# Sliding-window attention and gated MLP on one NeuronCore: 64-key score tiles, batched P V, and Q/K transposed on chip

## The chip, the core and the metric

The kernel runs on one NeuronCore of one Trainium2 chip. It is a whole transformer block in one launch: adaptive layer norm, attention in a sliding window, a second layer norm and a gated MLP, over 2048 tokens of width 640. The metric is device time in microseconds, the median of several runs. Names used below: TensorE (PE) multiplies matrices, PSUM is the memory it writes, in eight banks of 512 fp32 columns by 128 partitions; ScalarE (ACT) does the exponentials, VectorE (DVE) and GpSimd (POOL) work element by element, and SyncE (SP) issues the transfers.

## The reference

All values are bf16. `x` is 1 x 2048 x 640, there are 32 heads of 20 dimensions, and each query sees itself and the 255 tokens before it.

```python
mod = (silu(c) @ w_mod).reshape(1, 6, 1, -1)          # sa, ca, ga, sb, cb, gb
h = layernorm(x) * (1 + ca) + sa
x = x + ga * A(h, wqkv, wo)
h = layernorm(x) * (1 + cb) + sb
x = x + gb * B(h, w_gate, w_up, w_down)

def A(x, wqkv, wo):                                   # H = 32, Dh = 20, W = 256
    q, k, v = split(x @ wqkv)                         # by head
    scores = einsum('bhqd,bhkd->bhqk', q, k) * Dh ** -0.5
    mask = (idx[:, None] - idx[None, :] >= 0) & (idx[:, None] - idx[None, :] < W)
    p = softmax(where(mask, scores, -1e9))
    return merge(einsum('bhqk,bhkd->bhqd', p, v)) @ wo

def B(x, w_gate, w_up, w_down):                       # F = 1536
    return (sigmoid(x @ w_gate) * (x @ w_up)) @ w_down
```

## The kernel before

Every operation is recorded with an estimated duration, what it reads and writes, and a priority. A list scheduler then fixes the order of each engine's instructions ahead of time, and the order is emitted with semaphore waits. Buffers come from pools; a tile takes a slot when its first operation is placed. So the trace has one line for all untiled matmuls (L513) and one for the tiled ones (L514).

Pools and banks that matter here:

```python
CHUNKS = [2, 2, 4, 4, 4]                  # queries of a chunk, in blocks of 128
p_hT  = sbpool("hT", 2, [128, NDT, 512])  # x normalized and modulated, transposed
p_stg = sbpool("stg", 3, [128, 512])
p_QT  = sbpool("QT", 3, [128, 4, 512])
p_KT  = sbpool("KT", 4, [128, 4, 512])
p_V   = sbpool("V", 10, [128, H * VW + 10])
p_E   = sbpool("E", 4, [128, 4, 512])     # exponentials
p_S = Pool("S", [psum("S0", [128, 4, 512])])               # four banks: one score set
p_O = Pool("O", [psum("O0", [128, 512])])                  # one bank: P V
p_M = Pool("M", [psum(f"M{i}", [128, 512]) for i in range(3)])   # three banks: all else
```

Q and K are projected 512 tokens at a time with the dimensions on the partitions, then written to DRAM and read back so that four heads of a group lie at partitions 0, 32, 64 and 96:

```python
for mt in mts:                                        # 128 of the 640 dimensions
    pairs = [(ps, w[:, kt, mt * 128:(mt + 1) * 128], hT[cc].ap[:, kt, :]) for kt in range(NDT)]
    pe_chain(ps, 512, pairs, ...)
    evac(s, ps)                                       # PSUM to SBUF, ScalarE or VectorE
    dma(d[mt * 128:(mt + 1) * 128, :], s)             # to DRAM
for hh in halves:
    for j in range(4):                                # back, one head in four
        dma(t.ap[32 * j:32 * j + DH, :, :],
            d.rearrange("(g r) c -> r g c", r=4 * DH)[j * DH:(j + 1) * DH, 4 * hh:4 * hh + 4, :])
```

Attention goes group by group of four heads. A set is up to four pieces of 128 keys by 128 queries, so 512 columns in each of four banks. Scores use four row tiles of the array, P V four column tiles, directly after each other with a lag of two sets:

```python
for (kb, q0, n) in st:                                # scores: keys on 128 partitions
    for j in range(4):
        mm(Sp.ap[:, j, off:off + n * 128], kt.ap[32 * j:32 * j + DH, gl, keys of kb],
           qt.ap[32 * j:32 * j + DH, gl, queries], tp=(32 * j, 0))
activation(E.ap[:, :, 0:ncol], Sp.ap[:, :, 0:ncol], ACT.Exp, scale=SM_SCALE)
# diagonal and far blocks, on GpSimd:
affine_select(ap, ap, pattern=[[0, 4], [1, 128]], compare_op=ALU.is_ge, fill=0.0, ...)
for (kb, q0, n) in st:                                # P V
    for j in range(4):
        mm(O.ap[32 * j:32 * j + 32, oc:oc + n * 128], V[kb].ap[:, h * VW:h * VW + 32],
           E.ap[:, j, off:off + n * 128], tp=(0, 32 * j))
```

A full O bank is normalized on VectorE (transpose, reciprocal of the row sums, product, transpose back), goes to DRAM and comes back as the transposed input of the output projection. The MLP of a chunk computes gate and up for 128 of the 1536 hidden dimensions at a time, over all tokens of the chunk:

```python
for ft in range(NFT):
    for ps, w in ((pg, wg), (pu, wu)):
        pe_chain(ps, W, [(ps.ap[:, 0:W], w[:, kt, ft * 128:(ft + 1) * 128], h2.ap[:, kt, 0:W])
                         for kt in range(NDT)])
    activation(sg, pg, ACT.Tanh, scale=0.5)           # ScalarE
    scalar_tensor_tensor(hv(ft), sg, 1.0, pu, ALU.add, ALU.mult)   # VectorE
```

Of the kernel before, what the change touches and what calls it, by code (L numbers as in the profile page):

```python
# [13 lines left out]
D = 640  # L14
# [5 lines left out]
NG = H // 4  # L20
EPS = 1e-5
# [3 lines left out]
SWITCH = 0.094  # L25
ENGATTR = {"pe": "tensor", "act": "scalar", "dve": "vector", "pool": "gpsimd", "sp": "sync"}
ENGS = ("pe", "act", "dve", "pool", "sp")

# [44 lines left out]
class Op:  # L73
    __slots__ = ("engs", "eng", "fn", "dur", "lat", "deps", "succ", "tiles", "prio", "seq", "nleft", "ready", "start",
                 "end", "mode", "done", "key", "val", "signal", "nbytes", "k", "tmin", "isdma", "tag", "waits")


class Prog:
    def __init__(self, nc):
        self.nc = nc  # L80
        self.ops = []
        self.seq = 0

    def op(self, eng, fn, dur, reads=(), writes=(), prio=50.0, lat=0.06, nbytes=0, k=16, tmin=0.0, extra=(), tag="", hold=(), mode=0):
        o = Op()
        o.mode = mode
        o.engs = eng if isinstance(eng, tuple) else (eng,)
# [7 lines left out]
        o.isdma = nbytes > 0  # L95
        o.nbytes = nbytes
        o.k = k
# [42 lines left out]

    def schedule(self):
# [26 lines left out]

        for o in self.ops:
            if o.nleft == 0:  # L170
                arm(o)
        n = len(self.ops)
        placed = 0
        while placed < n:
            best = None
            for e in ENGS:
# [5 lines left out]
                for o in c.values():  # L182
                    st = max(free[e] + (SWITCH if e == "pe" and o.mode != pemode else 0.0), o.ready)
                    ok = True
                    for t in o.tiles:
                        if t.slot is None:
                            bs = None
                            for s in range(len(t.pool.tenant)):
                                rt = slot_time(t.pool, s)
                                if rt is not None and (bs is None or rt < bs):  # L190
                                    bs = rt
                            if bs is None:
                                ok = False
                                break
                            st = max(st, bs)
                        else:
                            for x in t.prev:
                                st = max(st, x.end + x.lat)
                    if ok:
                        lst.append((st, o))  # L200
                        if tmin is None or st < tmin:
                            tmin = st
                if not lst:
                    continue
                eps = 0.13 if e == "pe" else 0.04
                pick = min((x for x in lst if x[0] <= tmin + eps), key=lambda x: (x[1].prio, x[1].seq))
                ent = (pick[0], e, pick[1])
                if best is None or ent[0] < best[0]:
                    best = ent
# [8 lines left out]
            for t in o.tiles:  # L218
                if t.slot is None:
                    bs = None  # L220
                    for s in range(len(t.pool.tenant)):
                        rt = slot_time(t.pool, s)
                        if rt is not None and (bs is None or rt < bs[0]):
                            bs = (rt, s)
                    s = bs[1]
                    ten = t.pool.tenant[s]
                    t.prev = list(t.pool.init[s]) if ten is None else list(ten.rel)
                    t.slot = s
                    t.pool.tenant[s] = t
# [4 lines left out]
            free[e] = st + dur  # L234
            if o.isdma:
                s0 = max(st + dur + 1.2, bw)
                move = o.nbytes / 340e3
                bw = s0 + move
                o.end = s0 + max(move, o.nbytes / (o.k * 22e3)) + 0.9
# [12 lines left out]
            for t in o.tiles:  # L252
                t.left -= 1
                if t.left == 0:
                    last = {}
                    for x in t.ops:
                        if x.isdma:
                            last[x] = x
                        else:
                            last[x.eng] = x  # L260

# [12 lines left out]
    def emit(self):  # L274
# [6 lines left out]
        for e in ENGS:  # L281
            for o in self.order[e]:
# [4 lines left out]
                for d in ds:  # L287
                    if d is o:
                        continue
                    if d.eng == e and not d.isdma:  # L290
                        assert pos[d] < pos[o], (d.tag, o.tag)
                        if e in ("pe", "sp"):
                            continue
# [59 lines left out]
def c_pool(n):  # L353
    return 0.22 + n / 1150.0


def c_pe(n):
    return max(n, 64) / 2400.0 + 0.003


PVLAG = 2
MW = 100
CHUNKS = [2, 2, 4, 4, 4]


def build(nc, A_x, A_wqkv, A_wo, B_x, B_w_gate, B_w_up, B_w_down, c, w_mod, out, S=2048):
    NB = S // 128
    NCH = S // 512
# [18 lines left out]
    ident = sb("ident", [128, 128])  # L387
    c_col = sb("c_col", [128, NDT])
# [9 lines left out]
    p_x1 = sbpool("x1", 8, [128, D])  # L398
    p_hT = sbpool("hT", 2, [128, NDT, 512])
    p_h2 = sbpool("h2T", 1, [128, NDT, 512])  # L400
    p_stg = sbpool("stg", 3, [128, 512])
    p_QT = sbpool("QT", 3, [128, 4, 512])
    p_KT = sbpool("KT", 4, [128, 4, 512])
    p_V = sbpool("V", 10, [128, H * VW + 10])
    p_E = sbpool("E", 4, [128, 4, 512])
# [4 lines left out]
    p_oT = sbpool("oT", 1, [128, NDT, 512])  # L410
    p_big = sbpool("big", 1, [128, 6400])
    p_sig = sbpool("sig", 2, [128, 512], F32)
    p_st = sbpool("st", 3, [128, 64], F32)

    p_S = Pool("S", [nc.alloc_psum_tensor("S0", [128, 4, 512], F32)])
    p_O = Pool("O", [nc.alloc_psum_tensor("O0", [128, 512], F32)])
    p_M = Pool("M", [nc.alloc_psum_tensor(f"M{i}", [128, 512], F32) for i in range(3)])

    def R(name):
        return Res(name)  # L420

    R_wq, R_wk, R_wv, R_ident, R_ccol, R_cth, R_siluc, R_silubc = (
        R(n) for n in ("wq", "wk", "wv", "ident", "ccol", "cth", "siluc", "silubc"))
    R_wo = R("wo")
# [3 lines left out]
    R_mA, R_shB, R_scB, R_gbc, R_mh = R("mA"), R("shB"), R("scB"), R("gbc"), R("mh")  # L428
# [554 lines left out]
```

The softmax here doesn't subtract the row's maximum and nothing guards it: scores larger than these inputs give would overflow.

## Time and profile before

The median time is 378.63 us (378.45 to 379.73). The profiled execution took 378.4 us.

| | busy us | share of the span | instructions |
|---|---|---|---|
| TensorE matmuls | 344.5 | 91% | 3198 |
| TensorE weight loads | 172.9 | 46% | 3198 |
| ScalarE | 223.0 | 59% | 207 |
| VectorE | 218.8 | 58% | 471 |
| GpSimd | 177.0 | 47% | 281 |

| group | count | mean ns of one |
|---|---|---|
| exponential of 2048 elements, ScalarE | 80 | 1876 |
| exponential of 1536 elements, ScalarE | 8 | 1448 |
| mask selection of 512 elements, GpSimd | 240 | 662 to 665 |
| transposes of O, fp32 and back in bf16, VectorE | 32 and 32 | 714 and 707 |
| gate or up matmul of 512 columns | 360 | 386 to 387 |
| gate or up matmul of 256 columns | 240 | 273 |

How to read it: matmuls are pipelined, so the duration of one is longer than its distance to the next, and a busy TensorE isn't TensorE at its peak. The page cuts the span into 40 slices of 9.46 us and prints a digit for each, the busy share in tenths; a row of the same kind gives the clock that TensorE was granted. A line of a group names the source line, the engine, the operation, output <- input and the shapes. A line of the timeline gives start, duration, engine, operation and count, and in brackets how long the engine had been idle and what released it. Buffer numbers are left out of names.

### The profile page before, as it was taken

The numbers are of one execution on the slowest core, as the hardware profiler recorded it, in microseconds if no ns is written. First come the engines' busy times: TensorE is split into PE (matmuls) and PEld (weight loads), VectorE is DVE, ScalarE is ACT, GpSimd is POOL, SyncE is SP. The second block draws the span as 40 slices with busy tenths as digits, with TensorE's granted clock in tenths as the row PEclk, the third lists the DMA queues.
The fourth block names the chain that finished last, engine by engine and source line by source line (L and its number), as shares of the span: only waits on it lengthen the run. The fifth ranks groups of instructions, "written<-read, shape, count | busy, mean of one in ns | idle before, by whom it ended". The sixth has DMA issues, their size and how long they took to land.

```text
span 378.4 us, 8381 instructions
## 1 busy us (share of the span) xinstructions
PE 344.5 (91%) x3198; PEld 172.9 (46%) x3198; DVE 218.8 (58%) x471; ACT 223.0 (59%) x207; POOL 177.0 (47%) x281
## 2 busy tenths in 40 slices
PE   5796697678999799999999879999999999989996
PEld 2453243123445244655556423353554345744464
DVE  4354175767877755556886545397564638433332
ACT  1352366776888769878888767878778421012210
POOL 8111144679676845666668574667567300000000
PEclk9999699579999889999999969999999999999999
DMA  6999799976365042034203511200343020320001
GB/s 215 338 303 192 232 309 373 291 195 197 95 149 144 17 126 75 29 94 101 89 19 88 112 47 36 88 2 20 45 114 87 2 87 3 74 66 0 0 19 52
DMA packets 52887, 42.81 MB, mean 113 GB/s; under 512 B 22768, under 2 KB 49648, under 8 KB 52848
## 3 DMA queue, kind: packets, MB, share of 16 engines
q1 hardware_dynamic: 52848, 42.29, 41.0%
q8 instruction: 25, 0.41, 0.4%
q14 instruction: 14, 0.11, 0.1%
HBM read 27.20 MB, written 10.49 MB: 100 GB/s over the span
## 4 chain that ended last, share of the span: by engine, by line
PE 70%; DMA 8%; POOL 5%; ACT 5%; SPq 5%; issue 3%; DVE 2%; POOLq 0%
PE M L513 57%; PE S L514 7%; PE O L514 6%; SPq L435 5%; ACT E L755 4%; DMA KT<-dk 3%; POOL E L771 3%; DMA wo<-in_A_wo_dram 2%; DMA big<-in_w_mod_dram 1%; POOL E L773 1%; DMA oT<-doc 1%; DVE h2T L605 1%; POOL wo L920 0%; POOL wd L929 0%; DVE x L594 0%
## 5 line engine op out<-in xcount | busy, mean ns | idle before, releaser
L755 ACT ACTIVATE E<-S 128x2048 bf16<-128x2048 f32 (+1 forms) x96 | 169.8, 1769 | 39.5 <-PE S L514 37.0
L771 POOL TENSOR_SCALAR_AFFINE_SELECT E<-E 128x512 bf16<-128x512 bf16 x128 | 83.7, 665 | 99.8 <-ACT E L755 88.2
L773 POOL TENSOR_SCALAR_AFFINE_SELECT E<-E 128x512 bf16<-128x512 bf16 x112 | 72.9, 662 | 0.0
L882 DVE SCALAR_TENSOR_TENSOR big<-sig,M 128x512 bf16<-128x512 f32 (+1 forms) x60 | 34.6, 576 | 62.1 <-PE M L513 53.1
L513 PE MATMUL M<-h2T,wg 128*128 128x512 bf16 (+1 forms) x300 | 64.3, 341 | 1.9 <-DVE h2T L605 1.9
L880 ACT ACTIVATE sig<-M 128x512 f32<-128x512 f32 (+1 forms) x60 | 30.2, 512 | 59.0 <-PE M L513 58.8
L513 PE MATMUL M<-h2T,wu 128*128 128x512 bf16 (+1 forms) x300 | 63.7, 341 | 0.0
L513 PE MATMUL M<-wd,big 128*128 128x320 bf16 x384 | 55.7, 299 | 0.0
L514 PE MATMUL S<-QT,KT 20*128 20x128 bf16 (+2 forms) x768 | 39.0, 280 | 16.2 <-ACT E L755 11.7
L513 PEld LDWEIGHTS M<-wd,big 128*128 128x128 bf16 x384 | 36.4, 98 | 16.9 <-issue 3.0
L514 PE MATMUL O<-E,V 128*32 128x128 bf16 (+2 forms) x768 | 39.0, 282 | 1.7 <-DVE T L822 0.9
L513 PEld LDWEIGHTS M<-h2T,wg 128*128 128x128 bf16 x300 | 28.0, 98 | 26.4 <-issue 3.2
L513 PEld LDWEIGHTS M<-h2T,wu 128*128 128x128 bf16 x300 | 27.7, 99 | 25.3 <-issue 5.2
L514 PEld LDWEIGHTS S<-QT,KT 20*128 20x128 bf16 x768 | 11.7, 94 | 50.0 <-ACT E L755 34.8
L822 DVE STREAM_TRANSPOSE T<-O 128x512 f32<-128x512 f32 x32 | 22.9, 714 | 15.9 <-PE O L514 15.6
L513 PE MATMUL M<-hT,wq 128*128 128x512 bf16 x100 | 29.1, 433 | 2.2 <-DMA dk<-stg 1.6
L648 ACT ACTIVATE stg<-M 128x512 bf16<-128x512 f32 x28 | 16.7, 598 | 23.2 <-PE M L513 21.7
L892 DVE TENSOR_TENSOR x<-M,x 128x320 bf16<-128x320 f32 x32 | 15.7, 489 | 24.8 <-PE M L513 24.8
L583 DVE BATCH_NORM_STATS2 st<-x 128x6 f32<-128x320 bf16 x64 | 27.2, 473 | 3.9 <-DMA x<-in_A_x_dram 3.7
L513 PE MATMUL M<-wv,hT 128*128 128x320 bf16 x160 | 26.1, 306 | 1.1 <-DVE hT L605 1.1
L513 PE MATMUL M<-hT,wk 128*128 128x512 bf16 x100 | 25.7, 392 | 0.4 <-DMA dq<-stg 0.4
L513 PE MATMUL M<-wo,oT 128*128 128x320 bf16 x160 | 24.5, 300 | 1.1 <-DMA oT<-doc 1.1
(50 smaller groups left out, 255.5 us busy)
## 6 DMA issues: line engine op xcount, KB each, us to landing
x<-in_A_x_dram SPq DMA_DIRECT2D x32, 160.0 KB
big<-in_w_mod_dram SPq DMA_DIRECT2D x15, 320.0 KB
dq<-stg SPq DMA_DIRECT2D x20, 128.0 KB
dk<-stg SPq DMA_DIRECT2D x20, 128.0 KB
QT<-dq SPq DMA_DIRECT2D x32, 80.0 KB
KT<-dk SPq DMA_DIRECT2D x32, 80.0 KB
doc<-On SPq DMA_DIRECT2D x64, 40.0 KB
out_dram<-x SPq DMA_DIRECT2D x16, 160.0 KB
```

The source lines that it names most:

```text
L435: return e.dma_start(dst(), src())
L513: return e.matmul(o, l, r, start=st, stop=sp, skip_group_check=True)
L514: return e.matmul(o, l, r, start=st, stop=sp, tile_position=tp, skip_group_check=True)
L583: ins = e.bn_stats(v(bi * 12 + j * 6, 6), src[bi].ap[:, j * 320:(j + 1) * 320])
L648: return e.activation(dst(), src(), ACT.Copy)
L755: A("act", lambda e, eng, E=E, Sp=Sp, ncol=ncol: e.activation(E.ap[:, :, 0:ncol], Sp.ap[:, :, 0:ncol], ACT.Exp, scale=SM_SCALE), c_act(4 * ...
L771: return e.affine_select(ap, ap, pattern=[[0, 4], [1, 128]], compare_op=ALU.is_ge, fill=0.0, base=0, channel_multiplier=-1)
L773: return e.affine_select(ap, ap, pattern=[[0, 4], [-1, 128]], compare_op=ALU.is_ge, fill=0.0, base=-1, channel_multiplier=1)
L822: A("dve", lambda e, g: e.transpose(T1.ap[:], O.ap[:]), c_dve(512), reads=[O.r()], writes=[T1.r()], prio=4, tag="tr1")
L880: A("act", lambda e, g, pg=pg, sg=sg: e.activation(sg.ap[:, 0:W], pg.ap[:, 0:W], ACT.Tanh, scale=0.5), c_act(W), reads=[pg.r()], writes=[s ...
L882: A("dve", lambda e, g, pu=pu, sg=sg, ft=ft: e.scalar_tensor_tensor(out=hv(ft), in0=sg.ap[:, 0:W], scalar=1.0, in1=pu.ap[:, 0:W], op0=ALU. ...
L892: A("dve", lambda e, g, ps=ps, bi=bi, half=half: e.tensor_tensor(x1[bi].ap[:, half * 320:half * 320 + 320], ps.ap[:, 0:320], x1[bi].ap[:, ...
```

## The change

Queries go in eight chunks of 256 tokens, and the whole attention is laid out anew for them.

- Keys are taken 64 at a time. Two 64-key pieces lie side by side on partitions 0 to 63 and 64 to 127 of a score set, so that the scores use eight tiles of the array (32 rows by 64 columns), and the window of 256 is covered with less masked-out space. A chunk after the first has ten sets of 512 columns; the first has eight of 384.
- P V isn't done after each set. The five sets of four head groups are collected, and one burst computes their P V on eight tiles of 64 rows by 32 columns, in two phases: the two halves of the rows write different banks in each phase, and change over between them. TensorE waits for its own first phase (the fence). The O bank is gone; the burst takes two of now four M banks.
- Q and K are projected with tokens on the partitions, evacuated with 32 places a head, and transposed: by TensorE for the first three chunks, by transposing transfers for the others. The way through DRAM goes.
- Masks are kept as 0/1 tables and multiplied in, by VectorE or GpSimd, whichever the scheduler finds free first.
- The scheduler holds score sets to one per 3.2 us after the first chunk; projections run two chunks ahead; weights are loaded in another order, and the modulation weights borrow the room of other buffers.

The core of the diff, with cuts marked:

```diff
-CHUNKS = [2, 2, 4, 4, 4]
+CH = 256
+NPT = 3
+PACE0 = 15.0
+PACE = 3.2
+LEAD = 2
...
-    p_E = sbpool("E", 4, [128, 4, 512])
+    p_E = Pool("E", [Eall[:, i, :].rearrange("p (j c) -> p j c", j=4) for i in range(8)])
...
-    p_O = Pool("O", [nc.alloc_psum_tensor("O0", [128, 512], F32)])
-    p_M = Pool("M", [nc.alloc_psum_tensor(f"M{i}", [128, 512], F32) for i in range(3)])
+    p_M = Pool("M", [nc.alloc_psum_tensor(f"M{i}", [128, 512], F32) for i in range(4)])
...
+    def qkv(a, prio):
+        for bi in range(2):
+            for key, w, dst in (("q", "wq", QT[a]), ("k", "wk", KT[a])):
+                for half in range(2):
+                    pairs = [(ps.ap[:, 0:320], hT[a].ap[:, kt, bi * 128:(bi + 1) * 128],
+                              W3[w][:, kt, half * 320:half * 320 + 320]) for kt in range(NDT)]
+                    pe_chain(ps, 320, pairs, ...)
+                    evac(heads(s.ap[:, half * 512:half * 512 + 512], 32)[:, :, 0:DH], heads(ps.ap[:, 0:320], DH))
+                if a < NPT:
+                    for half in range(2):           # four matmuls of 128 columns with ident
+                        mm(e, ps.ap[:, i * 128:i * 128 + 128], s.ap[:, gi * 128:gi * 128 + 128], ident[:], ...)
+                else:
+                    transp_dma(dst.ap[:, :, bi * 128:bi * 128 + 128], s.ap[:])
...
+    def plan(a):
+        if a == 0:
+            for k in range(4):
+                sets.append(([(k, 0, 0, 4, 0), (k, 1, 2, 2, 4)], [(k, 0, 0, 4, 0), (k, 1, 2, 2, 4)], 6, ((0, "c"), (4, "c"))))
+            return sets
+        for k in range(4):
+            b = (k + 2) % 4
+            sets.append(([(k, 0, 0, 4, 0), (k, -1, 0, 3, 4), (k, -2, 0, 1, 7)],
+                         [(b, 0, 1, 3, 0), (b, -1, 0, 4, 3), (b, 1, 3, 1, 7)], 8, ((0, "d"), (6, "f"))))
+        sets.append(([(k, 1, 2, 2, 2 * k) for k in range(4)], [((k + 2) % 4, -2, 0, 2, 2 * k) for k in range(4)], 8,
+                     ((0, "2"),)))
...
+                    ins = mm(e, Sp.ap[64 * half:64 * half + 64, j, cu * 64:(cu + n) * 64],
+                             KT[kc].ap[32 * j:32 * j + DH, gi, kl:kl + 64],
+                             QT[a].ap[32 * j:32 * j + DH, gi, u * 64:(u + n) * 64], True, True, tp=(32 * j, 64 * half))
...
-                            return e.affine_select(ap, ap, pattern=[[0, 4], [1, 128]], compare_op=ALU.is_ge, fill=0.0,
-                                                   base=0, channel_multiplier=-1)
+                    return e.tensor_tensor(ap, ap, t.unsqueeze(1).to_broadcast([128, 4, w]), op=ALU.mult)
+            A(("dve", "pool"), mk, dur, reads=[E.r(), R_mk], writes=[E.r(cu)], prio=5, tag=f"mask{a}")
...
+    def burst(a, q, sets, Es):
+        X = [Tile(p_M, f"O{a}_{q}x"), Tile(p_M, f"O{a}_{q}y")]
+        phases = [(pick(0, (0, 1)), pick(1, (2, 3))), (pick(0, (2, 3)), pick(1, (0, 1)))]
...
+                    ins = mm(e, X[bank].ap[32 * j:32 * j + 32, oc:oc + n * 64],
+                             V[2 * a + kb].ap[64 * half:64 * half + 64, h * VW:h * VW + 32],
+                             E.ap[64 * half:64 * half + 64, j, cu * 64:(cu + n) * 64], ..., tp=(64 * half, 32 * j))
...
+            o = A("pe", ..., reads=list(rd), writes=[X[0].r(), X[1].r()], prio=8 - ph, mode=2, hold=X, fence=o)
...
-        for ft in range(NFT):
+        for f0 in range(0, NFT, 2):      # two hidden blocks of 256 tokens fill one bank
...
+    for a in range(NCH):
+        while nq < min(NCH, a + 1 + LEAD):
+            qkv(nq, 20 + nq)
+        oT = attention(a)
+        x1, h2 = outproj(a, oT)
+        mlp(a, x1, h2)
```

## Prediction

> **What bounds the kernel now.** I read the page first, its busy line and its forty slices.
>
> ```profile
> PE 344.5 (91%) x3198; PEld 172.9 (46%) x3198; DVE 218.8 (58%) x471; ACT 223.0 (59%) x207; POOL 177.0 (47%) x281
> ...
> PE   5796697678999799999999879999999999989996
> ...
> PEclk9999699579999889999999969999999999999999
> ```
>
> TensorE is the only engine near its span, and it has holes in the first nine slices (85 us) and hardly any later. The granted clock falls in the same slices. So I asked for the busy time of each engine in five stretches: before the first scores, until the first output projection, attention beside the MLP (two), and the MLP alone.
>
> ```profile
> 0.00:42.00 42.00, 29.82 (x221) 16.00 (x222) 17.80 (x50) 12.71 (x23) 12.23 (x24) 0.98 0.89 255
> 42.00:95.00 53.00, 42.71 (x453) 18.16 (x452) 34.94 (x73) 35.16 (x35) 31.65 (x43) 0.82 0.95 270
> 95.00:240.00 145.00, 137.63 (x1497) 69.41 (x1496) 94.89 (x203) 117.22 (x99) 94.41 (x152) 0.95 0.32 81
> 240.00:299.00 59.00, 59.00 (x595) 27.39 (x597) 36.61 (x76) 45.95 (x33) 37.45 (x61) 1.00 0.22 55
> 299.00:379.00 80.00, 75.38 (x441) 41.90 (x440) 34.58 (x70) 11.95 (x20) 1.27 (x2) 0.99 0.12 36
> ```
>
> The columns are TensorE, weight loads, VectorE, ScalarE, GpSimd, then granted clock, DMA share and GB/s. The stretch 42 to 95 runs at clock 0.82 with TensorE 81% busy and DMA 95% busy: attention has begun but no MLP is there to fill the gaps. The timeline says why it begins late, and the groups by tile say when the MLP begins:
>
> ```profile
> 15.87 3.52 PE L513 MATMUL M<-hT,wq 128*128 128x512 bf16 x15
> ...
> 41.22 0.51 PE L514 MATMUL S<-QT,KT 20*128 20x256 bf16 x8 [2.95 <-DMA KT<-dk]
> ```
>
> ```profile
> L513 PE MATMUL M<-h2T,wg x300: 272/379/634, 114.4 to 361.0; 128*128 128x512 bf16 x90, 128*128 128x256 bf16 x60
> ```
>
> From the first projection to the first score 25 us pass, in which Q and K go to DRAM and come back; the first gate matmul is at 114 us. Last, what attention costs TensorE where it is dense:
>
> ```profile
> 180.09 0.40 PE L514 MATMUL S<-QT,KT 20*128 20x384 bf16 x8
> 180.42 0.40 PE L514 MATMUL O<-E,V 128*32 128x256 bf16 x8
> 180.75 0.72 PE L513 MATMUL M<-h2T,wu 128*128 128x256 bf16 x5
> ```
>
> Each burst streams 512 columns on four tiles at once. Start to start it takes 0.33 us; the trace's untiled matmuls follow each other at 44 ns for 100 columns, 109 for 256 and 136 for 320, so a column is 0.417 ns and a matmul costs 2.5 ns more. 512 columns are 0.213 us; so about 0.11 us goes at each change of tile shape, three times a set (to scores, to P V, back). Inside a burst the four tiles start 3 to 4 ns apart, and the next round of four costs some 12 ns more than its columns.
>
> **TensorE's bill before.** Columns counted from the code: projections 153,600, scores and P V 92,160 (a quarter of the streamed ones, four run together), output projection 51,200, gate and up 245,760, down 122,880, modulation, warm-up and transposes 28,176: 693,776, or 288.9 us. Add 1,662 untiled matmuls at 2.5 ns (4.2), 96 sets at 3 x 0.11 (31.7) and second rounds (2.3): 327 us. The other 51 us are waiting and half clock: about 17 before 42 us, 17 from 42 to 95, 12 from 95 to 240, the rest start, end and the last MLP. (By stretch: start-to-start times of matmuls less this bill.)
>
> **What the Trainium skill says.** TensorEngine Tiling (Array Packing), section Key Properties: changing the tiling mode drains TensorE; the 0.11 us above agrees. TensorE: Matmul & The Clock Gate, Part 3, gives about 4 ns from one tile's start to the next; 3 to 4 ns here. Both allow eight tiles where there were four. The second page's section on the 56 ns gap also says that with hardware decode off the sequencer spends about 62 ns on each matmul. The trace can't decide it: its quickest long stretch has 62 matmuls in 2.85 us (46 ns each), which a queue filled beforehand could give, and over 150 matmuls it never goes below 80 ns. VectorE: DVE Perf Modes, section on the tier table, gives a bf16 product of two tensors two elements a cycle; the trace agrees, 128x640 takes 492 ns when undisturbed (wo scaling), but 803 median for the same shape beside busy GpSimd (wd).
>
> **The change, part by part.**
>
> *64-key score tiles.* A 256-query chunk covers five 64-key half-blocks per query instead of three whole 128 ones. Per chunk after the first, ten sets of 512 columns; eight of 384 in the first: 38,912 columns against 46,080, on eight tiles. That is 2 x 7,168 columns less for scores and P V, -6.0 us of TensorE. Exponentials: 70 x 1.876 + 8 x 1.448 = 142.9 us against 169.8, -27 us of ScalarE, off the path but in its favour.
>
> *P V in bursts.* 16 bursts of two phases. Shape changes: 78 x 2 + 16 x 2 = 188 against 288, 20.7 us against 31.7: -11.0. Extra rounds, two per set and about six per phase, 4.4 us against 2.3: +2.1; the wait of TensorE for its own first phase, about 0.15 each, +2.4.
>
> *Q and K by token.* Same 102,400 columns, 320 matmuls instead of 200. For three chunks 96 transposing matmuls of 128 columns: +5.1 us. 40 writes and 64 reads through DRAM go; 20 DMA transposes come for the later five chunks, hidden behind two chunks of lead.
>
> *256-token MLP.* Same columns, 960 matmuls for 600. With the projections and transposes 2,248 untiled matmuls, 5.6 us: +1.4. Transposes of x: +0.5.
>
> Sum: -6.0 - 11.0 + 2.1 + 2.4 + 5.1 + 1.4 + 0.5 = -5.5; the bill becomes about 322 us (693,008 columns, 288.8; 5.6; 20.7; 4.4; 2.4). So the arithmetic alone is worth 1.5%.
>
> *Start and filling.* This is the larger part. A first chunk of 256 tokens needs two x blocks instead of four ahead of the modulation weights, and the projections needed before its scores are 12,800 columns (5.3 us) and transposes, instead of a round trip of some 6 us. I put the first projection at 12 us and the first exponential near 22 (now 41.8). Eight exponentials of 1.45 us with their gaps end near 36, and output projection, layer norm and transposes bring the first MLP to about 50 us instead of 114. Until then chunks 1 and 2 give TensorE some 20 us of projections. After that scores are held to one set per 3.2 us, in which TensorE always has MLP work. Of the 51 us of waiting I leave: start until the first projection 9 (DMA brings 1.6 MB of w_mod by about 9.7 us[...]), 12 to 50 us 5, steady state 6, last MLP and end 4. That is 24, so -27 us.
>
> Prediction: 322 + 24 = 346 us, a ratio of 0.914.
>
> *The other engines.* Masks as products: per chunk 8 x (256 and 512 elements) and 2 x 2,048. At the two-element rate, with 155 ns fixed, 0.29 + 0.42 each and 1.22: 8.1 us, 63 us over the kernel if VectorE did all; GpSimd takes those that find VectorE busy, at two to three times the time (scaling a block of wd took it 1,467 ns, wo on VectorE 492). GpSimd's 157 us of mask selection goes. VectorE: 219 + about 40 of masks + 20 for more evacuations and modulations = 280 us, 81% of the new span. It becomes the second engine, and everything leaves TensorE's banks through it or ScalarE (about 210 us).
>
> **Rivals.**
>
> *The sequencer.* TensorE issues 1,920 score, 1,920 P V and 2,248 other matmuls: 6,088 against 3,198, one per 50 ns of the steady state (some 760 in a 38 us chunk). At 62 ns each they'd take 377 us, and the kernel about 390. For it: the skill's figure, and nothing denser in the trace than a queue could supply. Against: bursts start 3 ns apart, and the change's own model charges no such cost. About one in ten.
>
> *VectorE as the bound.* At 81% on average with in-order queues, O banks wait for transposes of 714 ns. Two of the four M banks then belong to a burst and the MLP lives on the other two. In the stretch 240 to 299 VectorE was 62% busy and TensorE never waited; in 95 to 240, 65%, and 12 us were lost. If this doubles or trebles the bubbles, 358 to 368 us. About one in five, in part.
>
> *Transfers hidden anyway.* Were the early stretch bound by DMA (95% busy from 42 to 95), moving Q and K off DRAM would free it: 5.2 MB written and 5.2 read. But weights of 2 MB each for gate, up and down still have to come in before the first MLP, behind 8.7 MB of others; at 270 to 340 GB/s, which the slices show, that is 43 us or more. If the MLP is late for it, 5 us more, 351.
>
> *Everything overlaps.* Bubbles vanish after the start: 332 us. This is the floor.
>
> **Range and chances.** Between the floor and a VectorE that costs 20 us more: 330 to 366 us. Faster by over 2% (under 371) needs only a third of the filling gain; only the sequencer or a starved TensorE beats it: 0.86. Within 2%: 0.05. Slower: 0.09.
>
> **What would show it.** First exponential near 22 us and first gate matmul near 50; no half clock after 50 us; score bursts about 0.35 us start to start although they have 24 matmuls; ScalarE's exponentials at 143 us; TensorE over 93% busy; VectorE near 280. I am wrong if score bursts last 0.6 us or more (eight tiles don't run together, or the sequencer binds), if TensorE's waits name VectorE's transposes of O, or if the first MLP still waits for weights at 70 us.

## The result, and the profile after

The changed kernel takes 367.83 us (median; 366.16 to 375.86) against 378.54 us for the kernel before, measured beside it. The ratio is 0.970, 95% interval 0.966 to 0.975. It is faster, as predicted, but by 11 us instead of 33, and outside the range of 330 to 366 us.

Two of its six executions (372.72 and 375.86 us) were in a slower state and are left out of the ratio, and the first profile is of one of them, so the changed kernel was run once more beside the first experiments. The views of "the kernel after" are of this repeat (370.48 us, 369.58 to 373.31; ratio 0.982, 0.972 to 0.992; profiled execution 368.1 us). First its busy line and three of the rows of forty slices:

```profile
PE 337.2 (92%) x6088; PEld 242.8 (66%) x6088; DVE 260.7 (71%) x543; ACT 219.1 (60%) x237; POOL 139.9 (38%) x160
...
PE   7698866999899899999999989899999999999996
...
DVE  5379997999769996855867599778668866432232
...
PEclk9999995999899999999999999999999999999999
```

TensorE has nearly twice the instructions and is still the busiest engine. VectorE is at 71%, less than I had foreseen, but its digits are 9 in slices 4 to 6, and TensorE's are only 6 to 8 in slices 4 to 7 (28 to 64 us). Busy time by stretch (TensorE, weight loads, VectorE, ScalarE, GpSimd, granted clock, DMA share, GB/s):

```profile
0.00:30.00 30.00, 24.80 (x253) 15.06 (x254) 16.57 (x40) 14.31 (x23) 10.69 (x44) 1.00 0.93 332
30.00:60.00 30.00, 20.60 (x432) 13.06 (x429) 29.48 (x53) 19.08 (x23) 23.49 (x19) 0.91 0.66 233
60.00:100.00 40.00, 36.63 (x717) 23.59 (x724) 35.77 (x84) 28.82 (x34) 23.35 (x22) 0.90 0.46 86
100.00:200.00 100.00, 94.74 (x2090) 66.66 (x2085) 74.98 (x167) 79.39 (x85) 44.33 (x40) 1.00 0.46 92
200.00:305.00 105.00, 100.15 (x2102) 74.55 (x2101) 79.99 (x159) 65.76 (x56) 37.06 (x33) 1.00 0.21 56
```

From 30 to 60 us VectorE is busy for 29.48 us of 30 and TensorE for 20.60, at clock 0.91. From 100 to 305 us TensorE is busy for 95% of the time. The attention itself is what the arithmetic said; here are a stretch of TensorE's timeline (start, duration, operation, count; lines between are left out) and the groups of the exponentials and of the first gate matmul:

```profile
175.77 0.43 PE L555 MATMUL S<-QT,KT 20*64 20x256 bf16 x24
176.24 1.73 PE L555 MATMUL M<-E,V 64*32 64x256 bf16 x128
177.94 0.84 PE L554 MATMUL M<-wo,oT 128*128 128x320 bf16 x5
...
185.82 0.43 PE L555 MATMUL S<-QT,KT 20*64 20x256 bf16 x24
186.18 1.05 PE L554 MATMUL M<-h2T,wu 128*128 128x256 bf16 x8
```

```profile
L795 ACT ACTIVATE E<-S x78: 1444/1877/1883, 24.6 to 290.8; 128x2048 bf16<-128x2048 f32 x70, 128x1536 bf16<-128x1536 f32 x8
...
L554 PE MATMUL M<-h2T,wg x480: 270/273/418, 94.9 to 357.4; 128*128 128x256 bf16 x160
```

A score burst of 24 matmuls is followed by the next kind 0.36 us after its start (185.82 to 186.18); 128 P V matmuls take 1.7 us. But the first gate matmul comes at 94.9 us, not near 50.

What VectorE does in its full stretch is seen in a group whose work is the same in every kernel here but b3, the normalization of x (one tensor, 128x640, with two scalars per row). By shape (busy, mean ns of one, then idle time before), beside the products on GpSimd:

```profile
L637 DVE TENSOR_SCALAR x<-x,st 128x640 bf16<-128x640 bf16 x32 | 25.1, 814 | 4.3 <-POOL st L634 4.3
L802 POOL TENSOR_TENSOR E<-E,mk 128x2048 bf16<-128x2048 bf16 x8 | 32.5, 4060 | 12.8 <-ACT E L795 12.7
L809 DVE TENSOR_TENSOR E<-E,mk 128x512 bf16<-128x512 bf16 x30 | 15.3, 509 | 1.5 <-ACT E L795 1.2
L809 POOL TENSOR_TENSOR E<-E,mk 128x512 bf16<-128x512 bf16 x26 | 31.1, 1198 | 17.1 <-ACT E L795 17.1
L982 POOL TENSOR_TENSOR wd<-wd,gbc 128x640 bf16<-128x640 bf16 x12 | 17.1, 1434 | 0.1
```

The normalization takes 441 ns in the median and 814 in the mean; the longest took 4,322 ns. The timeline shows what such long ones lie beside:

```profile
53.58 2.18 DVE L809 TENSOR_TENSOR E<-E,mk 128x256 bf16<-128x256 bf16 x2
...
54.04 2.97 POOL L982 TENSOR_TENSOR wd<-wd,gbc 128x640 bf16<-128x640 bf16 x2
55.68 2.70 DVE L637 TENSOR_SCALAR x<-x,st 128x640 bf16<-128x640 bf16 x2
...
58.44 1.03 PE L554 MATMUL M<-ident,x 128*128 128x128 bf16 x8 [4.99 <-DVE x L637]
...
122.62 4.63 DVE L637 TENSOR_SCALAR x<-x,st 128x640 bf16<-128x640 bf16 x2
122.66 4.05 POOL L802 TENSOR_TENSOR E<-E,mk 128x2048 bf16<-128x2048 bf16 x1 [0.60 <-ACT E L795]
```

At 122.6 us two normalizations that need 0.9 us last 4.6 us; GpSimd's product of 2048 elements covers all but the last half microsecond of it. At 55.7 us two last 2.7 us beside GpSimd's scaling of wd, after two masks that took 2.2 us. TensorE has waited 4.99 us when they end. VectorE's 29.48 busy microseconds of 30 are therefore not all work.

### The profile page after: what moved, and what is told of

The parts are those of the page before. It is cut to its first block, busy times and chain, and to the rows that moved or that the text cites. A ratio compares the mean times of both kernels' runs of the same rounds, so it can differ in the third digit from the quotient of the medians.

```text
span 373.7 us, 13956 instructions
## 1 busy us (share of the span) xinstructions
PE 338.6 (91%) x6088; PEld 243.6 (65%) x6088; DVE 266.5 (71%) x543; ACT 218.9 (59%) x237; POOL 140.2 (38%) x160
## 4 chain that ended last, share of the span: by engine, by line
PE 52%; ACT 2%; DVE 2%; issue 1%; POOL 0%; DVEq 0%; ACTq 0%
PE M L554 44%; PE M L555 4%; PE S L555 4%; ACT E L795 1%; DVE T L865 1%; ACT sig L932 0%; DVE On L872 0%; POOL E L809 0%; DVE hh L934 0%; DVE Tn L868 0%; ACT hT L651 0%; DVE x L946 0%; ACT V L696 0%; DVE Dr L866 0%; DVEq L337 0%
## 5 line engine op out<-in xcount | busy, mean ns | idle before, releaser
L795 ACT ACTIVATE E<-S 128x2048 bf16<-128x2048 f32 (+1 forms) x78 | 142.9, 1833 | 51.5 <-PE S L555 50.7
L809 POOL TENSOR_TENSOR E<-E,mk 128x256 bf16<-128x256 bf16 (+1 forms) x59 | 54.6, 937 | 96.8 <-ACT E L795 94.9
L554 PE MATMUL M<-h2T,wg 128*128 128x256 bf16 x480 | 64.0, 275 | 1.5 <-ACT h2T L651 0.8
L554 PE MATMUL M<-h2T,wu 128*128 128x256 bf16 x480 | 64.3, 276 | 1.0 <-DVE x L946 0.7
L934 DVE SCALAR_TENSOR_TENSOR hh<-sig,M 128x512 bf16<-128x512 f32 x48 | 32.6, 682 | 34.2 <-PE M L554 32.4
L932 ACT ACTIVATE sig<-M 128x512 f32<-128x512 f32 x48 | 28.6, 596 | 48.0 <-PE M L554 43.4
L554 PE MATMUL M<-wd,hh 128*128 128x320 bf16 x384 | 55.5, 299 | 1.0 <-DVE hh L934 0.7
L554 PEld LDWEIGHTS M<-wd,hh 128*128 128x128 bf16 x384 | 36.6, 98 | 16.1 <-DVE hh L934 1.3
L802 POOL TENSOR_TENSOR E<-E,mk 128x2048 bf16<-128x2048 bf16 x8 | 32.7, 4083 | 11.3 <-ACT E L795 11.2
L555 PE MATMUL S<-QT,KT 20*64 20x128 bf16 (+3 forms) x1920 | 33.6, 238 | 3.2 <-ACT E L795 1.9
L637 DVE TENSOR_SCALAR x<-x,st 128x640 bf16<-128x640 bf16 x32 | 28.9, 931 | 4.6 <-POOL st L634 4.6
```

Of the source, the lines that this page charges most:

```text
L554: return e.matmul(o, l, r, start=st, stop=sp, skip_group_check=True)
L555: return e.matmul(o, l, r, start=st, stop=sp, tile_position=tp, skip_group_check=True)
L637: A("dve", lambda e, g, bi=bi: e.tensor_scalar(dst[bi].ap[:], src[bi].ap[:], v(24 + 2 * bi, 1), v(30 + bi, 1), op0=ALU.subtract, op1=ALU.m ...
L795: A("act", lambda e, eng: e.activation(E.ap[:, :, 0:W], Sp.ap[:, :, 0:W], ACT.Exp, scale=SM_SCALE), c_act(4 * W), reads=[Sp.r()], writes=[ ...
L802: return e.tensor_tensor(ap, ap, mk_2.unsqueeze(1).to_broadcast([128, 16, 128]), op=ALU.mult)
L809: return e.tensor_tensor(ap, ap, t.unsqueeze(1).to_broadcast([128, 4, w]), op=ALU.mult)
```

## The experiments

**Theory.** GpSimd's long products of two tensors hold VectorE's instructions up while they run. In the early stretch VectorE gates every path, so this delay becomes TensorE's. The Trainium skill, page SBUF — State Buffer, section SBUF: two separate sides, says of the port pair through which VectorE and GpSimd both reach SBUF (the memory of their tiles) that it "is an exclusive lock, not a bandwidth split"; whoever holds it keeps the other out for the whole instruction. On VectorE's side it names operations in a two-port mode or with two inputs in SBUF. I had not put that into the prediction. **Rival 1:** VectorE simply has too much work of its own. **Rival 2:** the new order and the 256-token chunks do it, whatever engine masks.

The kernel before was measured beside each round of experiments. The rounds ran on four different chips, so kernels of different rounds are best compared by their ratios to it.

### Shortening products, order kept

In these runs the instructions stay in place and order, but some process only 4 elements; the masking they would do is left out.

```diff
 def mk(e, eng):
+    if eng == "pool":                        # a1; "dve" in a2; a3: only the 2048-element mask
+        ap = E.ap[:, :, cu*64:cu*64+1]
+        return e.tensor_tensor(ap, ap, t[:, 0:1]..., op=ALU.mult)
```

The repeat, and GpSimd's masks shortened (a1):

> The changed kernel as it is, for an undisturbed profile and as the reference of this group: 366 to 369 us. First gate matmul near 100 us in every theory, VectorE busy over 90% from 30 to 100 us.

> Order of instructions on every engine kept; each mask product that GpSimd does is cut to 4 elements (most of its masking is left out), which takes some 90 us of GpSimd's busy time and nothing of VectorE's own work. Theory A (GpSimd's two-input products hold up VectorE's instructions for as long as they last): VectorE's busy time falls by 25 to 35 us although its work is the same, the normalization of x falls from 931 ns mean to below 600, the first gate matmul comes before 90 us, and the time is 352 to 360 us. Rival B (VectorE has too much work of its own): VectorE's busy time falls by less than 8 us and the time by less than 3 us. Rival C (the early stretch waits for transfers or for the order that was fixed ahead): first gate matmul within 3 us of where it was, time within 4 us.

VectorE's masks shortened (a2), and only GpSimd's eight 2048-element ones (a3):

> Order kept; each mask product that VectorE does is cut to 4 elements (its masking is left out), which takes about 35 us of VectorE's own work and leaves GpSimd's. Theory A: part of the held-up time stays, 358 to 364 us. Rival B: as much as or more than the run without GpSimd's products, 348 to 357 us. Rival C: within 4 us of the changed kernel.

> Order kept; only the eight GpSimd products of 2048 elements (4.08 us each) are cut to 4. Theory A: the two normalizations of over 4 us disappear, VectorE is 8 to 12 us less busy, the wait of TensorE of some 5 us near 67 us goes, and the time falls by 4 to 8 us. Rivals B and C: less than 2 us.

| kernel | us | ratio (95%) | first gate matmul, us | normalization, mean ns | VectorE busy, us |
|---|---|---|---|---|---|
| a0, as changed | 370.48 | 0.982 (0.972 to 0.992) | 94.9 | 814 | 260.7 |
| a1 | 360.38 | 0.954 (0.944 to 0.963) | 92.7 | 452 | 237.5 |
| a2 | 362.97 | 0.960 (0.951 to 0.969) | 89.0 | 842 | 239.4 |
| a3 | 364.63 | 0.964 (0.954 to 0.975) | 93.5 | 573 | 248.3 |

In a1 no VectorE instruction was touched, and VectorE's busy time falls by 23.2 us. Its group of normalizations (as above):

```profile
L637 DVE TENSOR_SCALAR x<-x,st 128x640 bf16<-128x640 bf16 x32 | 13.5, 452 | 2.4 <-POOL st L634 2.4
```

So the lengthening is GpSimd's doing. The time, 10 us less, is just outside the 352 to 360 us that the theory gave, and the gate matmul moved by 2.2 us only, as the expectation has it for an order that was fixed ahead. But a2 brings 7.5 us by taking away VectorE's own work, which speaks for rival 1 as much, though its time lies in the theory's 358 to 364 us and not in that rival's 348 to 357. (The wait near 67 us that a3's expectation names stood in the first profile; the repeat has its long one at 58 us.) The intervals of a1, a2 and a3 overlap: this round shows the lengthening and doesn't settle the time. The next run shortens GpSimd's scaling products too (c1; the gates of wo and wd are then not applied), and a last one also VectorE's masks (e1; hardly any masking is left):

```diff
-A("pool", lambda e, g: e.tensor_tensor(wd[:, t, :], wd[:, t, :], gbc[:], op=ALU.mult), ...)
+A("pool", lambda e, g: e.tensor_tensor(wd[:, t, 0:4], wd[:, t, 0:4], gbc[:, 0:4], op=ALU.mult), ...)
```

(the same for wo)

> Order kept as in the changed kernel; GpSimd's mask products and its 17 products that scale wo and wd by the gate (1.44 to 1.48 us each, between 30 and 88 us) are all cut to 4 elements; most of both is left out. Theory A (held up by GpSimd's products of whatever purpose): VectorE's busy time falls a few us below the run with only the mask products cut, first gate matmul before 90 us, 354 to 358 us. Rival B (VectorE's own load): as that run, 359 to 362 us.

> Order kept as in the changed kernel; every mask product on either engine and GpSimd's scaling products are cut to 4 elements (masks and most of the scaling are left out). Against the run with only GpSimd's cut (355.7 us), VectorE loses another 30 us of own work. If VectorE's own load is the rest of the miss: 344 to 350 us and first gate matmul before 80 us. If the planned order is: 352 to 356 us.

c1: 355.74 us, 0.941 (0.935 to 0.946), gate matmul at 86.1, VectorE 229.0 us busy. VectorE's 543 instructions are those of the repeat, in the same order. c1's stretch from 30 to 60 us (columns as above):

```profile
30.00:60.00 30.00, 26.06 (x492) 16.35 (x490) 23.70 (x61) 22.20 (x27) 5.02 (x21) 0.89 0.72 253
```

The time without a matmul falls from 9.4 to 3.9 us there. Two groups by shape, the modulation of the MLP's input and the statistics of x, first in the repeat, then in c1:

```profile
L652 DVE TENSOR_SCALAR h2T<-h2T,scB,shB 128x256 bf16<-128x256 bf16 x25 | 13.3, 577 | 0.1
L627 DVE BATCH_NORM_STATS2 st<-x 128x6 f32<-128x320 bf16 x64 | 28.2, 472 | 1.7 <-DMA x<-in_A_x_dram 1.4
```

```profile
L652 DVE TENSOR_SCALAR h2T<-h2T,scB,shB 128x256 bf16<-128x256 bf16 x25 | 7.3, 338 | 0.3 <-DMA h2T<-x 0.3
L627 DVE BATCH_NORM_STATS2 st<-x 128x6 f32<-128x320 bf16 x64 | 28.3, 474 | 1.8 <-DMA x<-in_A_x_dram 1.5
```

So not every VectorE instruction is held up. The groups that get shorter in c1 are TENSOR_SCALAR from SBUF to SBUF (normalization 814 to 452 ns, modulation 577 to 338) and TENSOR_TENSOR with both inputs in SBUF (first chunk's masks 984 to 423). Statistics (472 and 474), transposes of O back (685 and 686) and evacuations of PSUM (CAST to stg, 483 and 489) last the same in both. That agrees with the lock, and not with a VectorE that is slowed as a whole.

e1: 354.89 us, 0.939 (0.933 to 0.944), gate matmul at 86.3, VectorE 211.4. With GpSimd's products gone, another 17.6 us of VectorE's own work is worth nothing that can be measured. So in this order VectorE's own load doesn't bound the kernel once GpSimd is quiet, and rival 1 falls in its plain form. By e1's own terms the rest of the miss lies in the planned order (352 to 356 us). That a2 gained nevertheless can be read so: as long as GpSimd's products take VectorE's time, any work taken off VectorE gives some back. That reading isn't isolated by a run.

### Moving the products to VectorE, full computation

Now nothing is left out; the scheduler plans anew, so the order changes as well.

```diff
-A(("dve", "pool"), mk, dur, ...)                 # b1
+A(("dve",), mk, dur, ...)
-A("pool", ... wo/wd[:, t, :] * gbc ...)          # b2 = b1 and this; d1 = this alone
+A("dve", ... wo/wd[:, t, :] * gbc ...)
```

> Full computation. All mask products on VectorE, order made anew for that. VectorE's own work rises by some 28 us, GpSimd's falls by about 95. Theory A: the time falls, 358 to 364 us. Rival B (own load): it rises or stays, 370 to 380 us.

> Full computation. As the last, and the scaling of wo and wd on VectorE as well (17 products at about 0.49 us against 1.45 on GpSimd): GpSimd does nothing large any more. Theory A: another 2 to 5 us less, 354 to 360 us. Rival B: slower than the last by some 2 us.

> Full computation. The changed kernel, masks shared between VectorE and GpSimd as it has them, with only the 17 scaling products of wo and wd moved from GpSimd to VectorE (8 us more of VectorE's own work, 25 us less of GpSimd's, all before 90 us). Theory A (GpSimd's long products hold up VectorE): 360 to 366 us. Rival B (VectorE's own load): 370 to 375 us.

b1 took 376.73 us, 0.996 (0.993 to 0.999): a clear miss, slower than the changed kernel. b2 took 360.29 us, 0.953 (0.946 to 0.960). d1 took 369.46 us, 0.979 (0.974 to 0.984), no better than the repeat (0.982). In b1 the scaling of wd is still GpSimd's, beside more VectorE work in the same stretch; by shape:

```profile
L982 POOL TENSOR_TENSOR wd<-wd,gbc 128x640 bf16<-128x640 bf16 x12 | 17.6, 1492 | 5.8 <-DVE st L629 5.8
L809 DVE TENSOR_TENSOR E<-E,mk_c 128x512 bf16<-128x512 bf16 x16 | 11.9, 781 | 0.3 <-ACT E L795 0.3
```

The first chunk's masks on VectorE take 781 ns in the mean there, and 416 in b2. So either half of the move alone brings nothing, and both together 6 to 11 us (0.953 against 0.970 and 0.982). That agrees with the lock, since each half leaves long products on both engines in the early stretch. But b1's normalizations take 451 ns, as if undisturbed, and yet it is slower than the repeat. These plans also differ in order, and I haven't separated that.

Relieving VectorE of the normalizations on top of b2, by giving them to ScalarE (917 ns each):

```diff
-A("dve", ... tensor_scalar(x, mean, rstd, op0=subtract, op1=mult) ...)
+A("act", ... activation(x, Identity, scale=rstd, bias=-mean*rstd) ...)
```

> Full computation. As the last, with the normalization of x (32 of 640 elements) moved to ScalarE and two small products per chunk more on VectorE. It takes 14 us of VectorE's own work and gives ScalarE about 22. Theory A: VectorE is no longer held up, so this is worth little, 353 to 360 us. Rival B: VectorE's load still counts, 4 to 8 us less than the last.

363.11 us, 0.961 (0.954 to 0.968); no gain over b2, and outside both ranges. VectorE is only 4.5 us less busy than in b2 (251.6 for 256.1) and each normalization takes 917 ns instead of 452, so this says little about VectorE's load. And the other way round, d1 with masks as selections on GpSimd (one tensor in, none of the masks on VectorE; the pieces differ by half of the partitions, so there are up to three per piece):

```diff
-A(("dve", "pool"), mk, dur, ...)                 # tensor_tensor with a 0/1 table
+A("pool", ... affine_select(half of the partitions) ...)     # 64 or 128 rows, 256 to 1024 elements
```

> Full computation. The last, with the masks back on GpSimd as selections (one input, no table), up to three per piece, since the two halves of the partitions need different bases; VectorE has no masks at all. Both theories expect less than the last: A 354 to 360 us, with the normalization of x still above 500 ns because selections of 0.4 to 1.2 us hold VectorE up too, B 350 to 356 us. If selections don't hold VectorE up, the normalization of x is near 440 ns.

360.91 us, 0.956 (0.950 to 0.961), just above the theory's range. GpSimd is busy for 196.7 us, more than in any other of these kernels, and yet this is 8.6 us better than d1. By shape:

```profile
L804 POOL TENSOR_SCALAR_AFFINE_SELECT E<-E 64x256 bf16<-64x256 bf16 x224 | 95.1, 425 | 54.9 <-ACT E L800 40.7 <-POOL st L639 0.6 <-PE M L559 0.5
...
L642 DVE TENSOR_SCALAR x<-x,st 128x640 bf16<-128x640 bf16 x32 | 17.6, 579 | 10.7 <-POOL st L639 10.4
```

The normalization's mean is 579 ns: selections hold VectorE up too, but less. Either that, or VectorE's own masks being gone (225.6 us busy against 262.9 in d1), can have given the gain: VectorE's masks were worth 7.5 us in a2, beside GpSimd's products, and nothing in e1, without them.

### Single parts of the change on the kernel before

Masks as products of either engine (p1), and 256-token chunks (p2), each put alone into the kernel before:

```diff
-A("pool", ... affine_select(E[128 keys, 4, 128]) ...)             # p1
+A(("dve", "pool"), ... tensor_tensor(E[...], mkt[...], mult) ...)
-CHUNKS = [2, 2, 4, 4, 4]                                          # p2
+CHUNKS = [2, 2, 2, 2, 2, 2, 2, 2]
```

> Full computation. The kernel before, with this part of the change alone: its 240 mask selections become products with a table, by VectorE or GpSimd, whichever is free first. Theory A: some 95 products of about 1.2 us stay on GpSimd and hold VectorE up, normalization of x above 650 ns; the time rises to 382 to 392 us. Rival B: VectorE has room (58% busy), 376 to 382 us.

> Full computation. The kernel before with 256-token attention and MLP chunks throughout, its scores, P V, projections and masks as they were. In all theories slower, since its 128-key sets then leave half-filled sets (more exponentials and more changes of tile shape): 384 to 396 us. If it is faster than 376, smaller chunks are by themselves what the change gains by.

p1 took 407.07 us, 1.080 (1.073 to 1.087): 30 us more than the kernel before beside it (407.07 - 407.07 / 1.080), worse than I expected. Its normalizations take 575 ns in the mean (539 in the kernel before), below the 650 that the theory gave. p2 took 390.59 us, 1.037 (1.028 to 1.046), 14 us more, as expected. By shape, p1's products:

```profile
L777 POOL TENSOR_TENSOR E<-E,mkt 128x512 bf16<-128x512 bf16 x95 | 114.7, 1210 | 138.4 <-ACT E L762 118.5 <-DVE T L826 8.3 <-PE M L520 7.3
L777 DVE TENSOR_TENSOR E<-E,mkt 128x512 bf16<-128x512 bf16 x145 | 102.1, 731 | 2.8 <-ACT E L762 2.7
```

145 products at 416 ns would be 60.3 us of VectorE; they last 102.1 at 731 ns. This part of the change, done alone, is a loss, in a kernel where VectorE was 58% busy before. How much of the 30 us is the lengthening, how much VectorE's 60 us of added work and how much the new order isn't separated.

### A plan with measured costs

Some entries of the scheduler's cost table were too small against the trace: modulation on ScalarE (0.43 for 590 ns), evacuations (0.45 and 0.43), the second phase of P V. On b2 I put these right (e3), then also held score sets to one per 3.5 us (e4), and last gave the mask and scaling products back to the engines that the changed kernel uses (e5).

```diff
-A(("dve", "act"), mo, {"dve": 0.33, "act": 0.43}, ...)            # e3, on b2
+A(("dve", "act"), mo, {"dve": 0.38, "act": 0.62}, ...)
-A(("act", "dve"), ev, {"act": 0.45, "dve": 0.43}, ...)
+A(("act", "dve"), ev, {"act": 0.60, "dve": 0.56}, ...)
-ncol / 2400.0 * 1.05 + 0.15 * ph
+ncol / 2400.0 + 0.12 + 0.23 * ph
-PACE = 3.2                                                        # e4 = e3 and this
+PACE = 3.5
-A(("dve",), mk, ...); A("dve", ... wo/wd * gbc ...)               # e5 = e4 and this
+A(("dve", "pool"), mk, ...); A("pool", ... wo/wd * gbc ...)
```

> Full computation. Masks and scaling on VectorE (360.3 us before), the order planned with measured costs of P V bursts and of ScalarE's and VectorE's modulations. If mis-sized costs made a bad order: 352 to 357 us. If not: 359 to 362 us.

> Full computation. As the last, scores held to one set per 3.5 us instead of 3.2. The chip gave sets 3.3 us apart on average whatever was planned, so a plan that asks for that lets VectorE keep up in the early chunks: 350 to 356 us. If the pace doesn't matter: as the last, within 2 us.

> Full computation. The changed kernel with its masks and scaling on both engines as they were, planned with the measured costs and 3.5 us. Theory A (GpSimd's products hold VectorE up): 364 to 370 us, no gain worth the name. If the order was the cause: 355 to 360 us.

e3 took 367.99 us, 0.971 (0.964 to 0.979): a miss, worse than b2, although its normalizations take 451 ns and GpSimd is busy for 21.4 us only. e4 took **352.33 us** (351.93 to 353.4), 0.932 (0.927 to 0.938), with the full computation: it beats both kernels. e5 took 377.12 us, 0.999 (0.997 to 1.002). e4's and e5's busy lines and two stretches (columns as above), e4 first:

```profile
PE 331.0 (95%) x6088; PEld 242.2 (69%) x6088; DVE 260.3 (74%) x639; ACT 214.7 (61%) x231; POOL 22.0 (6%) x70
...
30.00:60.00 30.00, 27.61 (x545) 18.03 (x543) 29.29 (x79) 23.94 (x31) 1.86 (x4) 1.00 0.75 255
60.00:100.00 40.00, 37.90 (x772) 26.28 (x771) 38.70 (x104) 32.99 (x37) 4.10 (x8) 1.00 0.59 110
```

```profile
PE 337.9 (90%) x6088; PEld 244.3 (65%) x6088; DVE 266.2 (71%) x551; ACT 215.5 (58%) x229; POOL 138.3 (37%) x160
...
30.00:60.00 30.00, 22.48 (x409) 13.22 (x406) 29.21 (x52) 18.22 (x22) 25.71 (x20) 0.94 0.65 233
60.00:100.00 40.00, 31.03 (x703) 20.62 (x704) 33.53 (x78) 29.34 (x32) 16.56 (x19) 0.87 0.31 64
```

VectorE is busy for the same 29 us of 30 in both. In e4 it gets 79 instructions done in them, in e5 52; TensorE gets 545 and 409. The normalizations take 449 ns in the mean in e4 and 870 in e5. With the same costs and the same pace, the engine of the masks and scalings makes 25 us (its own effect and that of the plan that follows from it). And e4 has VectorE 74% busy, as much as the changed kernel in microseconds (260.3 and 260.7), and is faster by 14 to 19 us (0.932 against 0.970 and 0.982): that load fits into 350 us where GpSimd doesn't interrupt it. But a quiet GpSimd isn't enough. e3, which differs from e4 in the pace alone, keeps TensorE busy for 32.04 us in the second stretch, where e4 has 37.90:

```profile
60.00:100.00 40.00, 32.04 (x845) 21.78 (x844) 36.95 (x98) 29.05 (x31) 3.44 (x8) 0.87 0.37 73
```

Nor do the sets keep one distance whatever is planned, as I wrote before e4: from the first exponential to the last they are 3.25 us apart in e3 and 3.48 in e4.

## Why the prediction was wrong

**TensorE's bill, 322 us: right within 5.** Score bursts take 0.36 us in the median with their change of shape (0.35 predicted), although most have 24 or 32 matmuls. A P V burst takes 1.66 us in the median; my terms (columns, rounds, a wait of 0.15 between phases) give about 1.4. The gap between the phases is 0.26 us. Redone with these: untiled work as predicted (615,184 columns at 0.417 ns and 2,248 starts at 2.5 ns, 261.9), the entry into 78 + 16 bursts at 0.11 (10.3), 78 x 0.359 (28.0) and 16 x 1.66 (26.6), together 327 us by this estimate. That is also the bill of before (where 693,776 columns are 289.1 us, not 288.9). So nothing is left of the 5.5 us that the arithmetic was to bring, and what was gained is waiting (51 us became 41).

**The sequencer rival: refuted.** e4 issues the same 6,088 matmuls in 350.0 us, 57 ns each over the whole span, and a burst issues 128 in 1.66 us, 13 ns each. The quickest 256 in a row of the repeat take 8.55 us, 33 ns each. No 62 ns apiece stands in the way.

**Exponentials: right.** 142.9 us, as worked out; the first at 24.6 us for 22 (the first projection at 15.3 for 12).

**The step that failed: the 24 us of waiting.** It is 368.1 - 327 = 41 us in the repeat. In c1, whose profiled execution took 353.2 us, it is 353.2 - 327 = 26, about what I had assumed; so 15 us go when GpSimd's products go, with the order kept. The term "12 to 50 us 5" is where most of it sits: 30 to 60 us alone has 9.4 us without a matmul, 3.9 in c1. The next is "steady state 6": from 100 to 305 us it is 10.1, and 6.2 in c1. The first chunk's exponentials do not end "near 36": the eighth starts at 43.1 us, and the first output projection comes at 66.9 (60.1 in c1, 57.1 in e4). The sentence behind it is "GpSimd takes those that find VectorE busy, at two to three times the time". I charged GpSimd's products to GpSimd, where there was room, and did not see that VectorE pays for them as well. The trace of before had shown it: I noted the scaling of wd at 803 ns "beside busy GpSimd" for 492 and took it as a price of that one row. Its normalizations, 441 ns in the median, show it too:

```profile
L594 DVE TENSOR_SCALAR x<-x,st 128x640 bf16<-128x640 bf16 x32 | 16.5, 539 | 3.0 <-POOL st L591 3.0
```

**The other marks.** TensorE is 92% busy for "over 93%", VectorE 260.7 us for "near 280". "No half clock after 50 us" is wrong: the granted clock is 0.91 from 30 to 60 and 0.90 from 60 to 100 us, at most 2.7 + 4.0 = 6.7 us of full clock lost, which are part of the 41. In c1 it is 0.89 and 1.00, in e4 1.00 in both.

**The first gate matmul at 50 us: wrong, but it costs less than I thought.** It comes at 81 us even in e4, and TensorE is nevertheless busy for 37.90 of 40 us there, with projections of later chunks. The mark was a bad one: the chunk's path through output projection, layer norm, transfers and modulation is longer than I allowed (in the repeat from 66.9 to 94.9 us, 28 us), but it is not what TensorE waits for as long as it has other work.

**VectorE as the bound, "358 to 368 us", "one in five, in part":** the size was right (367.83), and VectorE is what TensorE's longest wait from 30 to 100 us names (4.99 us). But the reason given was not right: its load was below my 280 us, O's transposes cost TensorE 0.6 us there, and the same load runs in 350 us in e4. So the size is in part luck. Of the transfers rival (351 us) the views show nothing: none of TensorE's waits from 30 to 100 us that I read names a weight of the MLP.

**Two parts of the change that I took for free are not.** Products for masks (p1) cost 30 us when alone; 256-token chunks (p2) cost 14 us. I had counted the first as load off the path and for the second's MLP 1.4 us. The effects don't carry over to the changed kernel: p2's sets of 128 keys make 120 exponentials for 96, where the change has 78, and each has an order of its own. So they are hints, and no measure of where a gain of 33 us shrank to 11.

**What stays open.** That GpSimd's products hold VectorE up, and that this costs the changed kernel's order time, is shown by c1: 14.7 us, or 11 to 16 by the ratios (0.941 against 0.970 and 0.982). What another order makes of it isn't settled. b1, d1 and e3 went against my numbers, and e3 and e4 differ by 16 us for a pace of 3.2 or 3.5. Without long products on GpSimd, the waiting by the same bill is 34 us in b2, 37 in e3 and 23 in e4. The replanned pair e4 and e5 gives 25 us. The last 6 us from e4 to the predicted 346 were not followed up.

## What to carry to other kernels

Before giving VectorE's spare products to GpSimd, count what each of them does to VectorE: here they cost 11 to 16 us in an order that was kept (c1), and 25 us with the order made anew (e5 against e4). Taking all of them on VectorE was better in b2 and e4, even where it was busy for 29 us of 30, but e3, which did the same in another order, was no faster than the changed kernel (0.971). A busy share can't tell work from being held up, so look for a group whose instructions all do the same and compare its median with its mean and maximum. Take one that can be held up: the statistics of x showed nothing here, the normalizations did. An order planned from a cost table needs the measured costs, and a run for each pace.

## What the runs showed of the hardware that I had not expected

- A VectorE instruction of 441 ns lasted up to 4,322 ns beside a GpSimd product of two tensors (4,060 ns for 2048 elements). In means over 32 instructions: 452 with GpSimd's masks shortened, 814 to 870 with them whole. The Trainium skill, page SBUF — State Buffer, section SBUF: two separate sides, describes this exclusion.
- GpSimd's product of two bf16 tensors takes 1,198 ns for 512 elements and 4,060 for 2048; VectorE's takes 416 and 1,222. The latter agrees with the two elements a cycle of the Trainium skill, page VectorE: DVE Perf Modes, section The perf-mode tier table, that I had cited (1,224 ns for 2048 there). The ratio of the engines is 2.9 to 3.3.
- The hold-up is selective: with GpSimd's products gone, VectorE's scalings of one SBUF tensor and products of two got shorter (577 to 338 ns, 984 to 423), its statistics, transposes and evacuations of PSUM did not (472 and 474, 685 and 686, 483 and 489).
- Selections on GpSimd, with one tensor in, hold VectorE up too (579 ns for the normalization in d3, beside selections of 64x256 that take 425 ns).
- TensorE takes 24 or 32 small matmuls on eight tiles in 0.36 us, with the change of tile shape, and waits 0.26 us for its own first phase in a P V burst.
